# Cosine attention and a GELU MLP in one kernel: scores and values share a ring of three PSUM bank pairs, score passes come in groups of 3,3,3,2,3,3,2,2, and one quad is transposed by TensorE

## Chip, core and metric

One core of one Trainium2 chip. The metric is the device time of one execution in microseconds (us), the median over the runs; lower is better.

## What is computed

```python
# q, k, v: (8, 12, 448, 64) float32; tau = 0.1
q_n = q / (np.linalg.norm(q, axis=-1, keepdims=True) + 1e-06)
k_n = k / (np.linalg.norm(k, axis=-1, keepdims=True) + 1e-06)
scores = np.matmul(q_n, k_n.transpose(0, 1, 3, 2)) / tau
attn = softmax(scores)
attn_out = np.matmul(attn, v)
# heads are put side by side: x is (3584, 768)
h = x @ w_in                                  # (768, 2048)
out = (0.5 * h * (1.0 + erf(h / sqrt(2)))) @ w_out   # (2048, 768)
```

There are 8 batches of 12 heads, 448 positions and 64 features. The output is 3584 rows of 768 float32.

## The kernel before

**Batches, quads, passes.** The kernel works batch by batch (b from 0 to 7). The 12 heads of a batch are three *quads* of four heads. The 448 keys of a head are cut into 7 chunks of 64. A *pass* is one chunk of one quad: `scores` (L227) issues four 64x64 matmuls of 448 columns, which run side by side in the four quarters of TensorE's array, into a tile `st` of two PSUM banks. `exps` (L238) has ScalarE read the two banks and write the exponentials (`pt`, bf16) to SBUF. A batch has 21 passes, 0 to 20; passes 0 to 6 belong to its first quad, 7 to 13 to the second, 14 to 20 to the third.

**Closing a quad.** When the seven passes of a quad have been exponentiated, `both` (L305) closes it. `sums` (L247) adds up the exponentials with a 128x32 matmul by ones into a bank `sm`. VectorE transposes that bank (`turned`, L275), inverts the sums (`inverted`, L280) and spreads them (`spread`, L296). `values` (L261) multiplies the exponentials with v into two banks `o`, again with four 64x64 matmuls side by side per chunk. `normalise` (L301), on VectorE, multiplies each `o` bank with the spread inverse into `x_t[b]`.

**The MLP.** `first` (L597) is the product `x @ w_in` of one batch: 96 matmuls of 128x128 weights and 448 columns, with the GELU on ScalarE into `g`. The product with `w_out` works on two batches at once: a tile of 128 rows and half of the 768 columns takes 16 matmuls of 384 columns (`second_pieces`, L323), then a VectorE copy (L336) into `ot`, then stores. These 16-matmul tiles are the *fill* of the next batch's attention: 96 matmuls (6 tiles) for batches 1, 3, 5 and 7, 128 (8 tiles) for 2, 4 and 6. Batch 0 has no fill and an order of its own, written out by hand (`attention_first`, L385). The tiles left at the end run alone.

**The order is written out by hand** (`manual_schedule`): each engine runs its instructions in the order of the calls, and semaphores keep the data right. `attention` (L563) says how batches 1 to 7 go: ten groups of two passes (group 0 is issued at the end of `first` of the batch before, the last group has one pass), with so many fill matmuls ahead of each group:

```python
plan = {96: (0, 18, 10, 10, 10, 0, 8, 8, 0, 8, 8, 16),
        128: (0, 22, 14, 14, 14, 0, 16, 16, 0, 8, 8, 16)}[len(fill)]
...
            if i in (5, 8):
                both(g0 + (0 if i == 5 else 1), 0 if len(fill) % KF else 1)
            group(b, i)
```

**PSUM's eight banks**: two pairs for `st` (a ring of two, `ps_st`), one bank for `sm` and one for the first half of `o` (`ps_acc`), and two that take turns for everything else (`mm_tile`, L96): the 16-matmul tiles, most of the products of `first`, the second half of `o`. The first products of `first` borrow `st` pairs.

**Preparing q and k.** SyncE's queue loads q and k of a quad (L122). GpSimd squares them (L149), VectorE adds the squares up (`reduce`, L158), ScalarE takes the root as exp(0.5 ln) (`logs`, `roots`), GpSimd adds 1e-6 (L183), VectorE inverts (L185), GpSimd scales and rounds to bf16 `qkb` (L201). A transposed copy `qkT` is then made: in batch 0 by TensorE and a VectorE copy (L218, L223), in the others by a DMA transpose that SyncE issues (L213). SyncE also issues the stores of the output; GpSimd issues the loads of v and of the weights. In the program a quad's preparation is a *unit*; unit 4 is quad 0 of batch 1, unit 5 its quad 1, unit 6 its quad 2.

Of the kernel before, what the change touches and what calls it, by code (L numbers as in the profile page):

```python
# [9 lines left out]
F32 = mybir.dt.float32  # L10
# [6 lines left out]
def kernel(  # L17
# [19 lines left out]
    C = S // D  # L37
    NQ = H // 4
# [4 lines left out]
    KF = d_ff // 128  # L43
# [14 lines left out]
    xp = ctx.enter_context(tc.tile_pool(name="xp", bufs=1))  # L58
    gp = ctx.enter_context(tc.tile_pool(name="gp", bufs=1))
    op_ = ctx.enter_context(tc.tile_pool(name="otp", bufs=3))  # L60
    ps_st = ctx.enter_context(tc.tile_pool(name="ps_st", bufs=2, space=bass.MemoryType.PSUM))
    ps_acc = ctx.enter_context(tc.tile_pool(name="ps_acc", bufs=1, space=bass.MemoryType.PSUM))
    ps_mm = ctx.enter_context(tc.tile_pool(name="ps_mm", bufs=1, space=bass.MemoryType.PSUM))

    ctx.enter_context(tc.manual_schedule())

# [29 lines left out]
    def mm_tile(name, shape=(128, 512), dtype=F32, aside=None):  # L96
        t = ps_mm.tile(list(shape), dtype, tag=f"mm{turn[0] if aside is None else turn[0] ^ aside}", name=name)
        if aside is None:
            turn[0] ^= 1
        return t  # L100

# [120 lines left out]

    st_t = {}

    def scores(g, banks):  # L227
        qkT = qkT_t[g]
        st = ps_st.tile([128, 2, 512], F32, tag="st", name=f"st{g}_{banks[0][1]}")
        for n, (s, c) in enumerate(banks):  # L230
            rows = slice(64 * s, 64 * (s + 1))
            for h in range(2):
                cols = slice(64 * h, 64 * (h + 1))
                nc.tensor.matmul(st[cols, n, :S], lhsT=qkT[rows, 1, c, cols], rhs=qkT[rows, 0, :, cols],  # L234
                                 start=True, stop=True, tile_position=(64 * s, 64 * h))
        st_t[g, banks[0]] = st
# [8 lines left out]
    bank_t = {}  # L245

    def sums(g, chunks=range(C)):  # L247
        for c in chunks:
            if c == 0:
                bank_t[g, "sm"] = ps_acc.tile([128, 512], F32, tag="sm", name=f"sm{g}")  # L250
            for s in range(2):
                if g < NQ:
                    nc.tensor.matmul(bank_t[g, "sm"][64 * s:64 * (s + 1), :S],  # L253
                                     lhsT=ones2.rearrange("p a h r -> p (a h r)"), rhs=pt_t[g, s, c],
                                     start=(c == 0), stop=(c == C - 1), tile_position=(0, 64 * s))
                    continue
                r = 32 * (2 * s + c % 2)
                nc.tensor.matmul(bank_t[g, "sm"][r:r + 32, :S], lhsT=ones, rhs=pt_t[g, s, c],  # L258
                                 start=(c < 2), stop=(c >= C - 2), tile_position=(0, r))

    def values(g, chunks=range(C), aside=None):  # L261
        for c in chunks:
            if c == 0:
                bank_t[g, 0] = ps_acc.tile([128, 512], F32, tag="o", name=f"o{g}_0")
                bank_t[g, 1] = mm_tile(f"o{g}_1", aside=aside)
            for s in range(2):
                for h in range(2):
                    rows, cols = slice(64 * h, 64 * (h + 1)), slice(64 * s, 64 * (s + 1))
                    nc.tensor.matmul(bank_t[g, h][cols, :S], lhsT=v_t[g][rows, s, c, :],  # L269
                                     rhs=pt_t[g, s, c][rows], start=(c == 0), stop=(c == C - 1),  # L270
                                     tile_position=(64 * h, 64 * s))
# [30 lines left out]
        b, n = divmod(g, NQ)  # L302
        nc.vector.tensor_tensor(x_t[b][:, 2 * n + h, :], bank_t.pop((g, h))[:, :S], rs_t.pop((g, h)), ALU.mult)  # L303

    def both(g, aside):  # L305
        sums(g)
        turned(g)
        inverted(g)
        spread(g, 0)
        spread(g, 1)  # L310
        values(g, aside=aside)
        normalise(g, 0)
        normalise(g, 1)

# [70 lines left out]
    def attention_first():  # L385
# [156 lines left out]
        spread(2, 0)  # L542
        inverses(4)
        scale(4)
        transposes(4)
        values(2, (2,))
        values(2, (3,))
        values(2, (4,))
# [4 lines left out]
        normalise(2, 1)  # L553
        done.update({square: 6, reduce: 5, root: 5, scale: 5, transposes: 5})

    passes = [(n, c) for n in range(NQ) for c in range(C)]

    def group(b, k):
        for n, c in passes[2 * k:2 * k + 2]:
            scores(b * NQ + n, ((0, c), (1, c)))  # L560
            exps(b * NQ + n, ((0, c), (1, c)))

    def attention(b, fill):  # L563
        fill = list(fill)
        plan = {96: (0, 18, 10, 10, 10, 0, 8, 8, 0, 8, 8, 16),
                128: (0, 22, 14, 14, 14, 0, 16, 16, 0, 8, 8, 16)}[len(fill)]

        def run(n):
            for _ in range(n):
                fill.pop(0)()  # L570

        x_t[b] = xp.tile([128, KD, S], BF16, tag="x", name=f"x{b}")
        g0, nu = b * NQ, (b + 1) * NQ + 1
        for i in range(1, 11):
            run(plan[i])
            if i == 1:
                for n in (nu - 1, nu):
                    upto(scale, n)
                    upto(transposes, n)
            if i in (5, 8):  # L580
                both(g0 + (0 if i == 5 else 1), 0 if len(fill) % KF else 1)
            group(b, i)
            if i in (2, 5):
                upto(square, nu + (1 if i == 2 else 2))
            if i in (6, 9):
                upto(reduce, nu + (1 if i == 6 else 2))
            if i == 3:
                upto(load_v, b + 3)
            if i == 3 and b == 1:
                upto(load_qk, g0 + NQ + 2)  # L590
            if i == 6:
                upto(load_qk, g0 + NQ + 3)
        upto(root, 2 * b + 5)
        run(plan[11])
        both(g0 + 2, 1)

    def first(b):  # L597
        sb, hf = divmod(b, 2)
        if hf == 0:
            g_t[sb] = gp.tile([128, KF, 2 * S], BF16, tag="g", name=f"g{sb}")  # L600
        nc.scalar.preload_act_table_set(GELU_SET)
        nu = (b + 1) * NQ + 1
        hps = {}
        pairs = (0, 2) if b else (0, 2, 6, 8)
        ahead = 4 if b else 5

        def mm(m, kds):
            for kd in kds:
                nc.tensor.matmul(hps[m], lhsT=wi[:, kd, m * 128:(m + 1) * 128],  # L609
                                 rhs=x_t[b][:, kd, :], start=(kd == 0), stop=(kd == KD - 1))  # L610

        def bank(m):
            if m in pairs:
                st = ps_st.tile([128, 2, 512], F32, tag="st", name=f"hp{b}_{m}")
                hps[m], hps[m + 1] = st[:, 0, :S], st[:, 1, :S]
            elif m not in hps:
                hps[m] = mm_tile(f"hp{b}_{m}")[:, :S]

        for m in range(ahead):
            bank(m)  # L620
            mm(m, range(KD - 2))
        if b == 0:
            upto(square, nu + 3)
        for n in (nu + 1, nu + 2) if b else (nu + 1,):
            upto(scale, n)
            upto(transposes, n)
        if b:
            upto(load_qk, (b + 1) * NQ + 5)
        else:
            upto(load_wo, 4)  # L630
        upto(square, nu + 3)
        upto(reduce, nu + 3)
        for m in range(ahead):
            mm(m, range(KD - 2, KD))
        for m in range(KF):
            if m >= ahead and (m == 0 or m - 1 not in pairs):
                for k in range(m, m + 1 + (m in pairs)):
                    bank(k)
                    mm(k, range(KD))
            nc.scalar.activation(g_t[sb][:, m, hf * S:(hf + 1) * S], hps.pop(m), AF.Gelu)  # L640
            if b == 0 and m == 5:
                nc.scalar.preload_act_table_set(EXP_SET)
                upto(root, 6)
                nc.scalar.preload_act_table_set(GELU_SET)
                upto(scale, nu + 2)
                upto(transposes, nu + 2)
                upto(load_qk, 2 * NQ + 1)
        if b + 1 < B:
            nc.scalar.preload_act_table_set(EXP_SET)
            group(b + 1, 0)  # L650
            upto(root, 2 * b + 6)
# [10 lines left out]
    fill = []  # L662
    for b in range(B):
        if b == 0:
            attention_first()
        else:
            attention(b, fill)
        first(b)
        sb, hf = divmod(b, 2)
        todo = [(t, ni) for t in (range(3) if hf == 0 else range(3, 7)) for ni in range(2)]  # L670
        if b == 0:
            todo.sort(key=lambda x: x[1])
        tail = [2 * S // 128 - 1] if b == B - 1 else []
        fill = [f for t, ni in todo if t not in tail for f in second_pieces(sb, t, ni)]
        fill += [f for t in tail for f in last_pieces(sb, t)]
# [37 lines left out]
```

## Time and profile before

| | |
|---|---|
| median of 13 runs | 427.48 us (426.58 to 436.22) |
| the profiled execution's own time | 427.85 us |
| its span, first to last instruction | 425.9 us |
| TensorE (PE) busy | 414.9 us, 97% |
| ScalarE (ACT) busy | 247.7 us, 58% |
| VectorE (DVE) busy | 191.8 us, 45% |
| GpSimd (POOL) busy | 166.5 us, 39% |
| granted TensorE clock | 0.999 |

The profile page gives busy times of the engines, a picture of the span in slices, the chain of work that ended last, and the costliest groups of instructions; the trace behind it can be asked for any stretch. Line numbers such as L234 are those of the kernel before. "st", "sm", "o", "hp" and "op" are the PSUM tiles of scores, sums, values, the first product and the second product. Stages of the span: batch 0's attention to 33.98 us, its `first` until the scores of batch 1 start at 54.33, batch 1's attention until 84.66, then `first` and attention in turns; the last `first` starts at 383.04 and the last 144 matmuls of the second product at 401.37.

### The profile page before, as it was taken

To read this page: it belongs to the slowest core of one execution; us is meant where nothing else is said; L and a number is where in the kernel's file an instruction comes from. 1 tells how busy PE (TensorE), PEld (TensorE's weight loads), DVE (VectorE), ACT (ScalarE), POOL (GpSimd) and SP (SyncE) were. 2 spreads that over 40 slices of the span, in tenths; PEclk is the share of its full clock that TensorE was granted. 3 is DMA by queue.
4 is the path that set the end of the run, shared out by engine and by line. 5 is a ranking of instruction groups with operands and counts; after the bars stand their busy time and mean duration, and the time that the engine had idled before them with its cause. 6 is when DMAs were issued, how large, how long until landed. Compare 5 with 4: busy or idle time off the path is not lost.

```text
span 425.9 us, 8166 instructions
## 1 busy us (share of the span) xinstructions
PE 414.9 (97%) x3448; PEld 208.6 (49%) x3448; DVE 191.8 (45%) x379; ACT 247.7 (58%) x356; POOL 166.5 (39%) x113
## 2 busy tenths in 40 slices
PE   7899989999999999999999999999999999999996
PEld 3344434555454554545454544555544455445564
DVE  6897117840288304941167501971048611562021
ACT  5895667546655467734767348745666357754300
POOL 5798706360813509090540906353180622000000
PEclk9999999999999999999999999999999999999999
DMA  8999999582482805655092642938076320320023
GB/s 287 269 251 203 176 182 302 123 198 79 84 210 51 225 37 101 172 118 180 17 215 76 129 168 21 228 87 232 2 122 184 82 43 2 82 55 21 2 74 75
DMA packets 68340, 54.99 MB, mean 129 GB/s; under 512 B 40400, under 2 KB 63312, under 8 KB 68304
## 3 DMA queue, kind: packets, MB, share of 16 engines
q1 hardware_dynamic: 55808, 42.25, 38.0%
q0 software_dynamic: 12112, 11.80, 18.1%
q8 instruction: 27, 0.44, 0.4%
q10 hardware_dynamic: 384, 0.43, 0.3%
q14 instruction: 9, 0.07, 0.1%
HBM read 45.61 MB, written 11.01 MB: 133 GB/s over the span
## 4 chain that ended last, share of the span: by engine, by line
PE 88%; POOL 4%; DMA 4%; issue 2%; DVE 1%; ACT 0%; POOLq 0%
PE op L332 35%; PE hp L609 30%; PE st L234 9%; PE o L269 8%; PE sm L258 4%; DMA qkT<-qkb 4%; POOL qkb L201 2%; PE op L347 1%; POOL wi L361 1%; POOL sq L149 1%; PE sm L253 0%; POOL v L134 0%; DVE x L303 0%; DVE nq L158 0%; ACT pt L241 0%
## 5 line engine op out<-in xcount | busy, mean ns | idle before, releaser
L241 ACT ACTIVATE pt<-st 128x896 bf16<-128x896 f32 x168 | 145.2, 915 | 51.2 <-PE st L234 51.0
L332 PE MATMUL op<-wo,g 128*128 128x384 bf16 x864 | 151.5, 327 | 0.0
L609 PE MATMUL hp<-x,wi 128*128 128x448 bf16 x768 | 146.8, 353 | 0.1
L640 ACT ACTIVATE g<-hp 128x448 bf16<-128x448 f32 x128 | 66.6, 547 | 94.9 <-PE hp L609 94.7
L332 PEld LDWEIGHTS <-g 128*128 128x128 bf16 x864 | 79.4, 98 | 66.7 <-issue 18.9
L609 PEld LDWEIGHTS <-wi 128*128 128x128 bf16 x768 | 74.5, 98 | 71.8 <-issue 3.2
L201 POOL TENSOR_TENSOR qkb<-qk,rn 128x896 bf16<-128x896 f32 (+1 forms) x48 | 77.9, 1650 | 10.3 <-DVE rn L185 10.3
L149 POOL TENSOR_TENSOR sq<-qk 128x1792 f32<-128x1792 f32 (+2 forms) x23 | 67.8, 2951 | 15.8 <-DMA qk<-in_k_dram 15.6
L336 DVE COPY ot<-op 128x384 f32<-128x384 f32 x54 | 29.6, 548 | 88.5 <-PE op L332 88.5
L183 POOL TENSOR_SCALAR se<-sr 128x28 f32<-128x28 f32 (+1 forms) x14 | 4.4, 312 | 165.2 <-ACT sr L174 165.2
L158 DVE TENSOR_REDUCE nq<-sq 128x28 f32<-128x1792 f32 (+2 forms) x30 | 48.8, 1636 | 30.0 <-POOL sq L149 29.8
L234 PE MATMUL st<-qkT 64*64 64x448 bf16 x672 | 53.1, 362 | 3.6 <-DMA qkT<-qkb 1.8
L185 DVE RECIPROCAL rn<-se 128x28 f32<-128x28 f32 (+2 forms) x18 | 6.9, 384 | 87.4 <-POOL se L183 87.2
L269 PE MATMUL o<-pt,v 64*64 64x448 bf16 x672 | 37.8, 352 | 0.0
L234 PEld LDWEIGHTS <-qkT 64*64 64x64 bf16 x672 | 17.7, 104 | 33.6 <-issue 24.7
L298 DVE STREAM_TRANSPOSE rs<-rc 128x448 f32<-128x448 f32 x48 | 28.2, 625 | 0.8
L303 DVE TENSOR_TENSOR x<-o,rs 128x448 bf16<-128x448 f32 x48 | 27.0, 599 | 0.6 <-DVE rn L185 0.3
L269 PEld LDWEIGHTS <-v 64*64 64x64 bf16 x672 | 18.3, 106 | 17.2 <-issue 9.1
L277 DVE STREAM_TRANSPOSE tr<-sm 128x448 f32<-128x448 f32 x24 | 15.5, 648 | 11.7 <-PE sm L258 11.1
L258 PE MATMUL sm<-pt,ones 128*32 128x448 bf16 x294 | 19.6, 355 | 0.0
L289 DVE TENSOR_REDUCE tr<-tr 32x28 f32<-32x28 f32 x84 | 16.5, 196 | 1.6
L258 PEld LDWEIGHTS <-ones 128*32 128x32 bf16 x294 | 6.9, 95 | 10.1 <-issue 6.6
(44 smaller groups left out, 117.6 us busy)
## 6 DMA issues: line engine op xcount, KB each, us to landing
out_dram<-ot SPq DMA_DIRECT2D x54, 192.0 KB, 2.8
qk<-in_q_dram SPq DMA_DIRECT2D x23, 448.0 KB, 5.8
qk<-in_k_dram SPq DMA_DIRECT2D x23, 448.0 KB, 6.4
v<-in_v_dram POOLq DMA_DIRECT2D x7, 672.0 KB, 9.5
wi<-in_moe_w_in_dram POOLq DMA_DIRECT2D x8, 384.0 KB, 11.3
wo<-in_moe_w_out_dram POOLq DMA_DIRECT2D x4, 768.0 KB, 16.8
qk<-in_q_dram SPq DMA_DIRECT2D x2, 224.0 KB, 3.5
v<-in_v_dram POOLq DMA_DIRECT2D x1, 448.0 KB, 8.8
```

The lines of the kernel that those rows point to most:

```text
L149: eng.tensor_tensor(sq[:, part], t[:, part], t[:, part], ALU.mult)
L158: nc.vector.tensor_reduce(nq[:, part], sq[:, part], mybir.AxisListType.X, ALU.add)
L201: eng.tensor_tensor(qkb[:, i, :, s0:s1].rearrange("p c s d -> p s c d"), t[:, i, s0:s1], rn[:, i].to_broadcast([128, s1 - s0, C, D]), ALU. ...
L234: nc.tensor.matmul(st[cols, n, :S], lhsT=qkT[rows, 1, c, cols], rhs=qkT[rows, 0, :, cols], start=True, stop=True, tile_position=(64 * s, 6 ...
L241: nc.scalar.activation(pt[:, :m], st[:, :m, :S], AF.Exp, scale=inv_tau)
L258: nc.tensor.matmul(bank_t[g, "sm"][r:r + 32, :S], lhsT=ones, rhs=pt_t[g, s, c], start=(c < 2), stop=(c >= C - 2), tile_position=(0, r))
L269: nc.tensor.matmul(bank_t[g, h][cols, :S], lhsT=v_t[g][rows, s, c, :], rhs=pt_t[g, s, c][rows], start=(c == 0), stop=(c == C - 1), tile_po ...
L298: nc.vector.transpose(rs, bank_t[g, "rc"][:, h].to_broadcast([128, NB, 32]))
L332: nc.tensor.matmul(ps[:, :NH], lhsT=g_t[sb][:, kf, t * 128:(t + 1) * 128], rhs=wo[:, kf, ni * NH:(ni + 1) * NH], start=(kf == 0), stop=(kf ...
L336: nc.vector.tensor_copy(ot[:, ni * NH:(ni + 1) * NH], ps[:, :NH])
L609: nc.tensor.matmul(hps[m], lhsT=wi[:, kd, m * 128:(m + 1) * 128], rhs=x_t[b][:, kd, :], start=(kd == 0), stop=(kd == KD - 1))
L640: nc.scalar.activation(g_t[sb][:, m, hf * S:(hf + 1) * S], hps.pop(m), AF.Gelu)
```

## The change

- Scores of batches 1 to 7 use three bank pairs in a ring, and a quad's two `o` banks are now one of these three pairs. The third pair is made, after batch 0's attention, from the two banks that `sm` and `o` had.
- `sums` of these batches goes into one of the two alternating `mm` banks: the one that the next tile would take, without moving the turn on.
- Groups have 3,3,3,2,3,3,2,2 passes; the plan has six runs of fill in place of nine. A quad is closed between groups 2 and 3, between 5 and 6, and after the last run.
- Batch 1's quad 0 (unit 4) is transposed by TensorE in `first` of batch 0 ahead of product m = 8, with two VectorE copies, in place of the DMA transpose that SyncE issued at the end of batch 0's attention.
- The calls that prepare later quads are put at the places of the new groups that come nearest to the old ones.

```diff
-    ps_st = ctx.enter_context(tc.tile_pool(name="ps_st", bufs=2, space=bass.MemoryType.PSUM))
-    ps_acc = ctx.enter_context(tc.tile_pool(name="ps_acc", bufs=1, space=bass.MemoryType.PSUM))
+    ps_st = ctx.enter_context(tc.tile_pool(name="ps_st", bufs=1, space=bass.MemoryType.PSUM))
     ps_mm = ctx.enter_context(tc.tile_pool(name="ps_mm", bufs=1, space=bass.MemoryType.PSUM))
+    acc = ctx.enter_context(ExitStack())
+    ps_acc = acc.enter_context(tc.tile_pool(name="ps_acc", bufs=1, space=bass.MemoryType.PSUM))
+    third = []
...
+    def pair(i, name):
+        pool = third[0] if i == 2 else ps_st
+        return pool.tile([128, 2, 512], F32, tag=f"st{i}", name=name)
...
             if c == 0:
-                bank_t[g, "sm"] = ps_acc.tile([128, 512], F32, tag="sm", name=f"sm{g}")
+                bank_t[g, "sm"] = ps_acc.tile([128, 512], F32, tag="sm", name=f"sm{g}") if g < NQ else \
+                    mm_tile(f"sm{g}", aside=0)
...
-            if c == 0:
+            if c == 0 and g < NQ:
                 bank_t[g, 0] = ps_acc.tile([128, 512], F32, tag="o", name=f"o{g}_0")
-                bank_t[g, 1] = mm_tile(f"o{g}_1", aside=aside)
+                bank_t[g, 1] = mm_tile(f"o{g}_1")
+            elif c == 0:
+                o = pair(p, f"o{g}")
+                bank_t[g, 0], bank_t[g, 1] = o[:, 0], o[:, 1]
...
         scale(4)
-        transposes(4)
...
     passes = [(n, c) for n in range(NQ) for c in range(C)]
+    group_pairs = [(0, 1, 2), (0, 1, 2), (0, 1, 2), (1, 2), (1, 2, 0), (1, 2, 0), (2, 0), (2, 0)]
 
     def group(b, k):
-        for n, c in passes[2 * k:2 * k + 2]:
-            scores(b * NQ + n, ((0, c), (1, c)))
+        n0 = sum(len(p) for p in group_pairs[:k])
+        for p, (n, c) in zip(group_pairs[k], passes[n0:]):
+            scores(b * NQ + n, ((0, c), (1, c)), p)
             exps(b * NQ + n, ((0, c), (1, c)))
...
-        plan = {96: (0, 18, 10, 10, 10, 0, 8, 8, 0, 8, 8, 16),
-                128: (0, 22, 14, 14, 14, 0, 16, 16, 0, 8, 8, 16)}[len(fill)]
+        plan = {96: (20, 12, 14, 12, 16, 22), 128: (24, 18, 20, 18, 22, 26)}[len(fill)]
...
+        run()
+        for n in (nu - 1, nu):
+            upto(scale, n)
+            upto(transposes, n)
+        group(b, 1)
+        upto(square, nu + 1)
+        run()
+        group(b, 2)
+        both(g0, 0)
+        upto(load_v, b + 3)
+        if b == 1:
+            upto(load_qk, g0 + NQ + 2)
+        group(b, 3)
+        upto(square, nu + 2)
+        run()
+        group(b, 4)
+        upto(reduce, nu + 1)
+        upto(load_qk, g0 + NQ + 3)
+        run()
+        group(b, 5)
+        both(g0 + 1, 1)
+        group(b, 6)
+        run()
+        group(b, 7)
+        upto(reduce, nu + 2)
         upto(root, 2 * b + 5)
-        run(plan[11])
+        run()
         both(g0 + 2, 1)
...
             if m in pairs:
-                st = ps_st.tile([128, 2, 512], F32, tag="st", name=f"hp{b}_{m}")
+                p = (2, 0)[m // 2] if b else (1, 0, 1, 0)[pairs.index(m)]
+                st = pair(p, f"hp{b}_{m}")
...
         for m in range(KF):
+            if b == 0 and m == 8:
+                for i in range(2):
+                    transposes(4, i)
+                    copies(4, i)
```

More of the change, by code (lines that the diff above doesn't have):

```diff
@@ L225, with scores @@
     st_t = {}
-    def scores(g, banks):
+    st_turn = [0]
+    def scores(g, banks, p=None):
         qkT = qkT_t[g]
-        st = ps_st.tile([128, 2, 512], F32, tag="st", name=f"st{g}_{banks[0][1]}")
+        if p is None:
+            p = st_turn[0]
+            st_turn[0] ^= 1
+        st = pair(p, f"st{g}_{banks[0][1]}")
         for n, (s, c) in enumerate(banks):
@@ L259, in sums, with values @@
                                  start=(c < 2), stop=(c >= C - 2), tile_position=(0, r))
-    def values(g, chunks=range(C), aside=None):
+    def values(g, chunks=range(C), p=None):
         for c in chunks:
-            if c == 0:
+            if c == 0 and g < NQ:
                 bank_t[g, 0] = ps_acc.tile([128, 512], F32, tag="o", name=f"o{g}_0")
-                bank_t[g, 1] = mm_tile(f"o{g}_1", aside=aside)
+                bank_t[g, 1] = mm_tile(f"o{g}_1")
+            elif c == 0:
+                o = pair(p, f"o{g}")
+                bank_t[g, 0], bank_t[g, 1] = o[:, 0], o[:, 1]
             for s in range(2):
@@ L303, in normalise, with both @@
         nc.vector.tensor_tensor(x_t[b][:, 2 * n + h, :], bank_t.pop((g, h))[:, :S], rs_t.pop((g, h)), ALU.mult)
-    def both(g, aside):
+    def both(g, p):
         sums(g)
@@ L310, in both @@
         spread(g, 1)
-        values(g, aside=aside)
+        values(g, p=p)
         normalise(g, 0)
@@ L564, in attention, with run @@
         fill = list(fill)
-        plan = {96: (0, 18, 10, 10, 10, 0, 8, 8, 0, 8, 8, 16),
-                128: (0, 22, 14, 14, 14, 0, 16, 16, 0, 8, 8, 16)}[len(fill)]
-        def run(n):
-            for _ in range(n):
+        plan = {96: (20, 12, 14, 12, 16, 22), 128: (24, 18, 20, 18, 22, 26)}[len(fill)]
+        parts = iter(plan)
+        def run():
+            for _ in range(next(parts)):
                 fill.pop(0)()
@@ L573, in attention @@
         g0, nu = b * NQ, (b + 1) * NQ + 1
[L574 to L592, printed above, removed]
+        run()
[23 more added lines that the diff above has]
+        upto(reduce, nu + 2)
         upto(root, 2 * b + 5)
-        run(plan[11])
+        run()
         both(g0 + 2, 1)
@@ L665 @@
             attention_first()
+            acc.close()
+            third.append(ctx.enter_context(tc.tile_pool(name="ps_third", bufs=1, space=bass.MemoryType.PSUM)))
         else:
```

## The prediction, made before the changed kernel was run

> **What bounds the kernel now.** I read the page's busy line first, then the chain that ended last, TensorE's waits, and the ACT and DVE timelines of one attention.
>
> ```profile
> PE 414.9 (97%) x3448; PEld 208.6 (49%) x3448; DVE 191.8 (45%) x379; ACT 247.7 (58%) x356; POOL 166.5 (39%) x113
> ```
>
> TensorE (PE) is the bound: 11 us idle of 425.9, and no other engine is near. So a gain must come out of PE's busy time. The chain shows where (start, length, what):
>
> ```profile
> 107.18 0.50 PE st L234 x8
> 107.68 2.38 PE op L332 x14
> 110.06 0.50 PE st L234 x8
> ...
> 401.37 15.60 PE op L332 x96
> ```
>
> The last stage gives an undisturbed fill matmul: 15.60/96 = 0.1625 us. A stream of 448 columns costs 0.19 (hp: 18.27/96), and the four matmuls of a pass run together. So the period 110.06 - 107.18 = 2.88 should be 14 x 0.1625 + 2 x 0.19 = 2.655. The rest, 0.225, is paid at the two joints between 128x128 and 64x64 work. With runs of ten (57.93 to 60.17: 2.24 - 2.005) it is 0.235: a fixed price per round trip, whatever the lengths. That is what fewer, larger groups can save.
>
> ```profile
> PE st L234 <- DMA qkT<-qkb: 1.8, 1, 1.8
> PE st L234 <- ACT pt L241: 1.2, 2, 1.0
> ```
>
> The first is batch 1's first pass, held to 54.33 by unit 4's DMA transpose (issued 38.37, 15.9 us to landing). The second is put down to ACT, but the exponentials had been done: pass 7 of batch 1 (63.68) waited for unit 5's transpose (issued 48.6, 15.0 to landing, so 63.6). Both crawl beside the w_out loads.
>
> **The joints, from start to start.** A fill run of n costs 0.1625n + 0.104 (16: 2.70). k passes cost 0.19k plus 0.125 between fills (107.11 to 107.61: 0.50), 0.12 ahead of sums, 0.10 behind values (118.48 to 118.96: 0.48). Sums take 0.864, values 1.348, or 1.45 ahead of hp. A batch with 128 fills before: 20.8 + 9 x 0.104 + 21 x 0.19 + 7 x 0.125 + 2 x 0.12 + 2 x 0.10 + 3 x 0.864 + (2 x 1.348 + 1.45) = 33.79; measured 33.90 (102.93 to 136.83), the rest a wait for an exponential. With 96 fills: 28.59; measured 29.13 (155.09 to 184.22), the rest two such waits and 0.30 at 173.3 for an mm bank that a VectorE copy still held; 28.84 in batch 7. The terms close, so I trust them.
>
> **After, without new waits.** Six runs in place of nine; four groups between fills in place of seven; two ahead of sums and two behind values as before. That is 3 x (0.104 + 0.125) = 0.69 less: 33.09 and 27.89.
>
> **New waits, three, each from rows.** Durations hold; only the order is new.
>
> ```profile
> 155.20 0.55 ACT L640 ACTIVATE g<-hp 128x448 bf16<-128x448 f32 x1 [0.59 <-PE hp L609]
> 155.76 1.28 ACT L649 ACT_TABLE_LOAD   x1
> 157.06 1.73 ACT L241 ACTIVATE pt<-st 128x896 bf16<-128x896 f32 x2
> 158.67 0.32 ACT L165 ACTIVATE lq<-nq,tiny 128x28 f32<-128x28 f32 x1
> 159.08 0.23 ACT L174 ACTIVATE sr<-lq 128x28 f32<-128x28 f32 x1
> 159.21 1.71 ACT L241 ACTIVATE pt<-st 128x896 bf16<-128x896 f32 x2
> ```
>
> (1) Quad 0 closes right behind group 2, whose first pass is its last (pass 6). The exponential starts 0.44 after the pass, lasts 0.92 and is seen 0.05 later: 1.41. Sums reach their seventh chunk at 0.69 + 0.55 = 1.24 (four chunks' matmuls side by side, three rounds ahead). Wait 0.17 per batch.
> (2) With 96 fills ACT is behind already. After hp's end it needs the GELU and the table load and starts pass 0 at 1.96 (157.06 - 155.09), then one per 0.81, with 0.67 for the two root steps behind pass 2: pass 5 ends at 1.96 + 2.43 + 0.67 + 1.62 + 0.92 = 7.60. PE wants its bank pair for pass 8 at 0.69 + 3.35 + 0.69 + 2.05 + 0.40 = 7.18. Wait 0.4 here, in which (1) is hidden. Batches 1 and 7 have no root steps there and pay (1).
> (3) Sums now use an mm bank, so quad 2's wait for the copy of the last tile but one, and that copy stands in VectorE's queue behind a reduce and a root:
>
> ```profile
> 173.50 0.64 DVE L277 STREAM_TRANSPOSE tr<-sm 128x448 f32<-128x448 f32 x1
> ...
> 176.73 1.12 DVE L303 TENSOR_TENSOR x<-o,rs 128x448 bf16<-128x448 f32 x2
> 177.77 2.00 DVE L158 TENSOR_REDUCE nq<-sq 128x28 f32<-128x1792 f32 x1
> 179.69 0.55 DVE L336 COPY ot<-op 128x384 f32<-128x384 f32 x1
> 181.34 0.50 DVE L185 RECIPROCAL rn<-se 128x56 f32<-128x56 f32 x1 [1.10 <-POOL se L183]
> 182.01 0.56 DVE L336 COPY ot<-op 128x384 f32<-128x384 f32 x1 [0.17 <-PE op L332]
> ```
>
> From quad 1's sums VectorE needs 0.98 to start, 4.27 through normalise, 0.48 a copy, 2.0 reduce, 0.1, 1.15 for the root through ACT and POOL, 0.48 reciprocal, 0.56 copy, 0.03: 10.05. PE comes from sums to sums in 0.864 + 1.348 + 0.48 + 2.70 + 0.505 + 3.68 = 9.58 with 96 fills: wait 0.47. With 128 it takes 11.2: none. Batch 7 has no such root: none. Behind each of these waits stands all later work of PE, so each is paid in full. Others do not bind. Pair 0 is wanted for pass 13 at 13.38 after the batch's start, free at 13.26 (quad 0's sums start at 7.91, plus 0.98 and 4.37; VectorE has nothing else queued). The next tile in sums' bank comes 2.7 after sums start, and the bank is read by 1.63. Quad 1's sums, at 16.36 with 96 fills, want a copy that stands behind the first reduce (13.13 to 15.1) and ends at 15.6; without that 0.75 of cover they wait one to one. hp's last k-steps want x 5.35 after quad 2's sums start and normalise ends at 5.33, as before. The squares, loads and reduces that are called a pass or two earlier or later lie on POOL and SP, where batch 3's last squares ended 15.6 after its start and their reduce comes at 22: nothing, while that cover of 6 holds.
>
> **Batch 1 and the transposes.** Fourteen TensorE transposes are added where PE is the bound. In batch 0 seven take 0.40 from start to next (18.07 to 18.47), 56 ns each. The Trainium skill ("TensorE: Matmul & The Clock Gate", Part 4: PE-mode transpose) gives about 275 ns each in one kernel's context, and with that they would cost 3.85 us and eat what batch 1 gains. In this trace about 220 ns is one transpose's length, but they overlap; I take 0.8, with 3.9 as the far end (below nothing is excluded: nothing hides work on the bound). The two VectorE copies (0.62 each) start when a reciprocal is over (45.16) and end at 45.8 and 46.4; hp 10 and 11 want the banks at 46.2 and 47.3, so hp's own matmuls hide them by 0.4; if that cover went, hp would slip by as much. POOL's order is unchanged. On SP's queue the move frees unit 5's transpose, unit 7's loads and unit 6's transpose.
> Unit 5's packets, by the trace, ran 53.5 to 63.1, behind unit 4's (42.35 to 53.5), near 185 a us while wo loads ran. Without unit 4, wo moves 200 instead of 145 KB a us and ends near 58.4 instead of 61; unit 5 (1792 packets) starts near 51.5 and lands near 60. Pass 7 wants it at 33.98 + 18.26 + 0.8 + 7.0 = 60.0. Bounds: no wait, to 3.5 if it lands at 63.6 as now. I take 0.2. Unit 7's squares then come before the reduce that stands ahead of the copy for quad 1's sums.
> From hp's start to the end of batch 1: before 33.98 to 84.66 = 50.68. After 18.26 + 0.8 + 27.89 + 0.17 + 0.1 (pass 5's bank) + 0.47 + 0.2 = 47.89. Gain 2.8.
>
> **The sum.** Batch 1: 2.8. Batches 3 and 5: 29.13 - (27.89 + 0.4 + 0.47) = 0.37 each. Batch 7: 28.84 - 28.06 = 0.78. Batches 2, 4, 6: 33.90 - (33.09 + 0.17) = 0.64 each. Total 2.8 + 0.74 + 0.78 + 1.92 = 6.2. Profiled time 427.85 - 6.2 = 421.65; the median lies 0.37 lower: 421.3. The `first` stages and the tail do not change.
>
> **Rivals.**
> *More of it comes free* (0.12): waits (1) to (3) do not appear, because ACT or VectorE get through sooner. Then 6.2 + 3 x 0.17 + 2 x 0.87 + 0.17 + 0.94 = 9.6 less: 417.9. Against: the same rows reproduce the before to 0.1.
> *Unit 5 is as late as ever* (0.15): wo takes the freed share and pass 7 waits until 63.6. It waits 3.6 in place of 0.2 and of (1), so batch 1 loses 0.4 instead of gaining 2.8: 424.5. For it: transposes got only about a quarter of the traffic while wo ran.
> *It doesn't do what it says* (0.08): the 0.23 belongs to the pass, not to the joint (a third pass costs 0.3). Then the joints are not saved and (1) to (3) come on top: batches 2, 4, 6 lose 0.06 each, 3 and 5 lose 0.33 each, 7 gains 0.08, batch 1 gains 2.1: 426.2. Against: behind values a pass costs 0.19.
> *Slower* (0.05): one VectorE queue holds a PE bank. Place: quad 2's sums in batches 1 to 6. Wait (3) grows one to one with any delay of reduce or root: three batches at once, the 128-fill ones from 1.15 on. Slower by 0.5% (8.3 us lost) takes 2 us more in each. The point: the last unit's squares end after 24 us of the batch; they ended at 15.6. Price then: 430.
>
> The likeliest case has 0.60. Below 0.5% (2.1 us) nothing can be told from no change here. Range 418.9 to 424.8: it takes in the last transpose case and most of the free one. Faster 0.86, same 0.09, slower 0.05.
>
> **What would show it.** Right: st groups of three at 0.69 between fills, runs of 12 at 2.05, batch 2's attention 33.25 and batch 3's 28.75; PE st waiting on DMA qkT gone or below 1 us; transposes 0.8 us ahead of hp 8; sm of quad 2 waiting 0.5 for the copy (L352 of the changed kernel) in batches 1, 3 and 5 only; sums' last chunk waiting 0.17. Wrong: a third pass at 0.3; waits of o or op for DVE in the 128-fill batches; unit 5 landing after 61; attention stages equal to before.

## The result and the profile after

The changed kernel's median is 420.97 us (11 runs), the kernel before 427.15 us in all runs beside it: ratio 0.9858, interval [0.983, 0.9887]. Forecast: 421.3. Faster, by the amount and in the places forecast, with a few terms off.

The changed kernel's profiled execution took 423.26 us (span 421.5), longer than the median, and the reason must be read off first. From the page: TensorE's busy line and the granted clock in 40 slices.

```profile
PE 413.1 (98%) x3462; PEld 213.5 (51%) x3462; DVE 190.1 (45%) x381; ACT 245.8 (58%) x356; POOL 166.5 (39%) x113
PEclk9799999999999999999999999999999999999999
```

The second slice has a 7 where the kernel before had nines throughout. Two stretches of it (from and to, length, busy us and count of PE, PEld, DVE, ACT and POOL, then granted clock, DMA share, GB/s):

```profile
12.00:16.30 4.30, 2.90 (x29) 1.68 (x28) 2.69 (x6) 3.89 (x7) 1.19 (x3) 1.00 1.19 277
16.30:23.10 6.80, 6.80 (x39) 2.46 (x35) 4.53 (x7) 4.65 (x7) 6.76 (x7) 0.50 1.09 282
```

For 6.8 us in batch 0, TensorE had half its clock, and batch 0 ended at 36.56 instead of 33.98. Its order of work is the same in both kernels, and in the seven profiles below it ended between 33.3 and 33.8. So 2.6 us of the profile belongs to this execution, not to the change, and everything is compared by stages from batch 0's end on. Stage times here are from the first matmul of a stage to that of the next, in us:

| kernel | batch 0's product and batch 1's attention | attention 2, 4, 6 | attention 3, 5 | attention 7 |
|---|---|---|---|---|
| before | 20.35 + 30.34 = 50.69 | 33.90 | 29.13 | 28.84 |
| forecast | 47.89 | 33.26 | 28.76 | 28.06 |
| after | 19.04 + 28.41 = 47.45 | 33.24 | 28.52 | 28.21 |

The other seven product stages are 18.26 (the last 18.17) in both. From the start of batch 0's product to the last attention's end the changed kernel saves 3.24 + 3 x 0.66 + 2 x 0.61 + 0.63 = 7.1 us.

TensorE's timeline of batch 2's attention after (start, length with the overlap of the last matmul, count), which answers to the chain lines of before:

```profile
106.97 0.76 PE L246 MATMUL st<-qkT 64*64 64x448 bf16 x12
107.67 3.10 PE L348 MATMUL op<-wo,g 128*128 128x384 bf16 x18
110.70 0.76 PE L246 MATMUL st<-qkT 64*64 64x448 bf16 x12
111.39 1.08 PE L271 MATMUL sm<-pt,ones 128*32 128x448 bf16 x14
112.40 1.52 PE L285 MATMUL o<-pt,v 64*64 64x448 bf16 x28
113.75 0.55 PE L246 MATMUL st<-qkT 64*64 64x448 bf16 x8
114.23 3.42 PE L348 MATMUL op<-wo,g 128*128 128x384 bf16 x20
```

Read the starts. Three passes take 0.70 (106.97 to 107.67) where two took 0.50: the third costs 0.19, the bare stream, and the joint is paid once. Eighteen fills take 3.03 = 18 x 0.1625 + 0.104. Sums take 1.01 in place of 0.864 (111.39 to 112.40): wait (1).

TensorE's waits in the changed kernel (two of five lines; the other three lie in batch 0):

```profile
PE st L246 <- ACT pt L253: 1.1, 1, 1.1
PE sm L271 <- DVE ot L352: 0.6, 3, 0.2
```

The waits for a DMA transpose are gone from the list. The first line is one wait in batch 0 (at 12.7), a few us ahead of the halved clock. The second is wait (3), three times. The waits of 0.1 to 0.2 for exponentials are not listed: they hide inside the busy time of overlapping matmuls, and only the distance from start to start shows them.

### The profile page after: what moved, and what is told of

The parts are those of the page before. It is cut to its first block, busy times and chain, and to the rows that moved or that the text cites. A ratio compares the mean times of both kernels' runs of the same rounds, so it can differ in the third digit from the quotient of the medians.

```text
span 421.5 us, 8166 instructions
## 1 busy us (share of the span) xinstructions
PE 413.1 (98%) x3462; PEld 213.5 (51%) x3462; DVE 190.1 (45%) x381; ACT 245.8 (58%) x356; POOL 166.5 (39%) x113
## 4 chain that ended last, share of the span: by engine, by line
PE 47%; issue 29%; POOL 18%; DMA 2%; DVE 2%; SPq 1%; ACT 1%; POOLq 0%
PE hp L633 17%; PE op L348 15%; POOL sq L156 9%; POOL qkb L208 8%; PE st L246 5%; PE o L285 4%; DMA qk<-in_k_dram 2%; PE sm L271 2%; PE sm L266 1%; PE op L363 1%; PE tp L225 1%; POOL v L141 1%; POOL se L190 1%; SPq L129 1%; PE spin L399 0%
## 5 line engine op out<-in xcount | busy, mean ns | idle before, releaser
L253 ACT ACTIVATE pt<-st 128x896 bf16<-128x896 f32 x168 | 142.9, 917 | 42.5 <-PE st L246 41.9
L348 PE MATMUL op<-wo,g 128*128 128x384 bf16 x864 | 147.9, 327 | 0.0
L348 PEld LDWEIGHTS <-g 128*128 128x128 bf16 x864 | 81.1, 98 | 63.7 <-issue 13.2
L246 PE MATMUL st<-qkT 64*64 64x448 bf16 x672 | 48.9, 362 | 1.3 <-ACT pt L253 1.1
L285 PE MATMUL o<-pt,v 64*64 64x448 bf16 x672 | 36.9, 352 | 0.0
L246 PEld LDWEIGHTS <-qkT 64*64 64x64 bf16 x672 | 18.6, 105 | 27.6 <-issue 19.7
L271 PEld LDWEIGHTS <-ones 128*32 128x32 bf16 x294 | 7.8, 95 | 11.5 <-issue 8.0
```

Of the source, the lines that this page charges most:

```text
L253: nc.scalar.activation(pt[:, :m], st[:, :m, :S], AF.Exp, scale=inv_tau)
L348: nc.tensor.matmul(ps[:, :NH], lhsT=g_t[sb][:, kf, t * 128:(t + 1) * 128], rhs=wo[:, kf, ni * NH:(ni + 1) * NH], start=(kf == 0), stop=(kf ...
```

## Experiments

Seven kernels, made from before or after (e6 from e4). The ratio is to the runs of before beside each kernel (medians 426.77 to 427.13). Stages of the profiled execution, in us:

| kernel | product 0 + attention 1 | 2, 4, 6 | 3, 5 | 7 | median | ratio to before, interval |
|---|---|---|---|---|---|---|
| e1_groups_only | 19.97 + 31.85 | 33.24 | 28.50 | 28.21 | 423.3 | 0.9914 [0.988, 0.9948] |
| e2_transpose_only | 19.05 + 29.17 | 33.90 | 29.12 | 28.83 | 424.98 | 0.9955 [0.9942, 0.9968] |
| e3_ring_groups_of_two | 19.05 + 28.87 | 33.90 | 28.81 | 28.81 | 424.15 | 0.9933 [0.9908, 0.9958] |
| e4_sums_in_pair | 19.05 + 28.16 | 33.24 | 28.21 | 28.21 | 419.73 | 0.9827 [0.9788, 0.9866] |
| e5_one_more_reduce | 19.05 + 29.10 | 33.24 | 29.15 | 28.21 | 422.57 | 0.989 [0.9852, 0.9928] |
| e6_sums_in_pair_and_plan | 19.05 + 28.04 | 33.24 | 28.04 | 28.04 | 419.16 | 0.9825 [0.9779, 0.9871] |
| e7_reduce_ahead | 19.05 + 31.54 | 34.10 | 31.83, 32.07 | 28.21 | 433.48 | 1.0148 [1.0113, 1.0183] |

**e1_groups_only: is the TensorE transpose worth anything?** From after:

```diff
         scale(4)
+        transposes(4)
...
-            if b == 0 and m == 8:
-                for i in range(2):
-                    transposes(4, i)
-                    copies(4, i)
```

> The changed kernel with one part undone: unit 4 is transposed by SyncE's DMA again, at its old place; groups, ring and banks stay as changed. My account: the joints are saved in all seven batches, but in batch 1 the first pass is held to the landing of unit 4's transpose (54.3 us, if batch 0 runs as in the profile of before) and pass 7 to unit 5's (63.6); that batch ends near 84.9 instead of 81.4, so about 424.4 us. Rival, that the transposes were hidden anyway and all of the gain is in the groups: about 421 us, no TensorE wait on a DMA above 1 us.

Measured 423.3, with every batch from 2 on as in the change. From TensorE's waits, then its timeline in batch 1:

```profile
PE st L246 <- DMA qkT<-qkb: 3.3, 2, 1.9
```

```profile
60.12 0.38 PE L246 MATMUL st<-qkT 64*64 64x448 bf16 x4
62.38 0.57 PE L246 MATMUL st<-qkT 64*64 64x448 bf16 x8 [1.88 <-DMA qkT<-qkb]
62.88 1.16 PE L271 MATMUL sm<-pt,ones 128*32 128x448 bf16 x14
63.97 2.83 PE L285 MATMUL o<-pt,v 64*64 64x448 bf16 x28
```

Both transpose waits are there, as expected, and pass 7 waits longer than before, since the larger groups reach it sooner. New is the last line: values took 2.62 from start to next in place of 1.35. No semaphore holds them; the granted clock was 0.5 from 63.5 to 66.9, and that belongs to this execution: its mean clock was 0.995, while the other five of e1 had 0.998 to 1.0, and 3.4 us at half clock take 0.004 off the mean. Without the 1.3 us that values lost by it, batch 1 would have come to about 50.5, as before (50.69). So without the moved transpose the larger groups gain nothing in batch 1, and 421 needs both parts. The rival falls.

**e2_transpose_only: the other part by itself.** From before: the same four lines moved the other way (`transposes(4)` out, the block ahead of m = 8 in).

> The kernel before with the other part alone: unit 4 transposed by TensorE ahead of product m = 8; groups of two, two pairs, own banks for sums and values. My account: the product stage of batch 0 grows by 0.86 us and the two transpose waits (2.1 with the pass's idle time, and 1.05) go; 427.15 - 2.3 = about 424.9 us, and batches 2 to 7 to the hundredth as before (33.90 and 29.13). Rival, that it matters only together with larger groups: 427 us.

Measured 424.98: the product of batch 0 and batch 1's attention take 48.22 instead of 50.69, 2.5 less, and all later stages stay within 0.01. The part pays alone.

**e3_ring_groups_of_two: banks or joints?** The three pairs with the old plan, from after:

```diff
-    group_pairs = [(0, 1, 2), (0, 1, 2), (0, 1, 2), (1, 2), (1, 2, 0), (1, 2, 0), (2, 0), (2, 0)]
+    pass_pairs = [0, 1, 2, 0, 1, 2, 0, 1, 2, 0, 2, 0, 2, 0, 1, 2, 1, 2, 1, 2, 1]
...
-        plan = {96: (20, 12, 14, 12, 16, 22), 128: (24, 18, 20, 18, 22, 26)}[len(fill)]
+        plan = {96: (0, 18, 10, 10, 10, 0, 8, 8, 0, 8, 8, 16),
+                128: (0, 22, 14, 14, 14, 0, 16, 16, 0, 8, 8, 16)}[len(fill)]
```

with the loop of before around it, `both` at groups 5 and 8, and values in pairs 1, 0 and 0.

> The changed kernel's three bank pairs, values in a pair, sums in an mm bank, transposes on TensorE, but the old plan: groups of two passes and nine runs of fill. My account (the gain is in the joints, 0.23 each, not in the banks): batches 2, 4, 6 stay at 33.8 to 33.9, batches 3 and 5 at 28.9 to 29.3, only batch 1 gains; about 424.5 us. Rival (the third pair takes waits for exponentials away, which hide inside busy TensorE time): batches 2 to 7 gain what they gained in the change, 33.24 and 28.5; about 421 us.

TensorE in batch 2 of this kernel:

```profile
100.06 3.75 PE L348 MATMUL op<-wo,g 128*128 128x384 bf16 x22
103.74 0.57 PE L246 MATMUL st<-qkT 64*64 64x448 bf16 x8
104.24 2.45 PE L348 MATMUL op<-wo,g 128*128 128x384 bf16 x14
106.62 0.57 PE L246 MATMUL st<-qkT 64*64 64x448 bf16 x8
```

A period of 2.88 (103.74 to 106.62), the one of the kernel before, to the hundredth, with the third pair there. Batches 2, 4 and 6 stay at 33.90. The third pair by itself is worth nothing there; in batches 3 and 5 it takes 0.32 away, the wait that values had for an mm bank. What the change saves is joints. Groups of three with only two pairs were not run; that they need the third pair is an estimate: the third pass would want the first one's bank 0.38 after the first one's start, and that bank is read by 1.36 (the exponential starts 0.44 after the pass and lasts 0.92).

**e4_sums_in_pair: wait (3) taken away.** Quad 2's sums in pair 2 instead of an mm bank, from after:

```diff
-                    mm_tile(f"sm{g}", aside=0)
+                    (mm_tile(f"sm{g}", aside=0) if p is None else pair(p, f"sm{g}")[:, 0])
...
-        both(g0 + 2, 1)
+        both(g0 + 2, 1, 2)
```

> The changed kernel with quad 2's sums in the first bank of pair 2 (its pass 19 has been read long before) instead of the mm bank that a copy behind reduce and root still holds; nothing else. My account: the wait of 0.24 to 0.30 us ahead of these sums in batches 1, 3 and 5 goes, nothing else comes (the first product of the next stage wants pair 2 only 2.3 us after sums start, and the bank is read by 1.7); 0.8 us less than the changed kernel, about 420.2 us. Rival, that the wait moves to the next thing behind VectorE's queue (values' pair or the products' last k-steps): the same 421 us, with hp waiting on VectorE.

TensorE around quad 2 of batch 3, after and then e4:

```profile
176.00 3.75 PE L348 MATMUL op<-wo,g 128*128 128x384 bf16 x22
179.98 0.93 PE L271 MATMUL sm<-pt,ones 128*32 128x448 bf16 x14 [0.23 <-DVE ot L352]
```

```profile
172.52 3.75 PE L348 MATMUL op<-wo,g 128*128 128x384 bf16 x22
176.20 0.93 PE L271 MATMUL sm<-pt,ones 128*32 128x448 bf16 x14
```

From 3.98 to 3.68 start to start, and 28.52 to 28.21 for the stage; nothing took the wait's place. Of the 420.97 - 419.73 = 1.24 us by medians, the stages show 0.25 + 2 x 0.31 = 0.87. Taken each against the runs of before beside it, the medians agree: 426.77 - 419.73 = 7.04 saved against 427.15 - 420.97 = 6.18, so 0.86.

**e5_one_more_reduce and e7_reduce_ahead: the slower rival made large.** One more VectorE reduce of 2 us, of squares already there, into a tile that nobody reads; e5 puts it behind the second reduce, e7 ahead of it:

```diff
         upto(reduce, nu + 2)
+        if nu + 2 <= NU:
+            again = nrm.tile([128, 2, 2, C], F32, tag="again", name=f"again{b}")
+            nc.vector.tensor_reduce(again, sq_t[units[nu + 1][0]], mybir.AxisListType.X, ALU.add)
         upto(root, 2 * b + 5)
```

> The changed kernel with one more VectorE reduce of 2 us (into a tile that nobody reads) right behind the second reduce of batches 1 to 6, so ahead of the root, the last copies and quad 2's sums: it makes the slower rival's mechanism larger. My account: the copy that quad 2's sums wait for comes 1.93 us later; with 96 fills the wait of 0.24 to 0.30 grows by all of it, with 128 fills VectorE's way (9.88 in the changed kernel's batch 3) had 1.3 left to TensorE's 11.2, so 0.6 appears. 3 x 1.93 + 3 x 0.6 = 7.6: about 428.5 us, batch 3 at 30.45 and batch 2 at 33.85. Rival, that VectorE has slack enough (45% busy) to hide 2 us: 421 us.

Measured 422.57: my account missed by 6 us. VectorE's timeline in batch 3, after and then e5:

```profile
175.83 2.00 DVE L165 TENSOR_REDUCE nq<-sq 128x28 f32<-128x1792 f32 x1
179.02 0.50 DVE L192 RECIPROCAL rn<-se 128x56 f32<-128x56 f32 x1 [1.19 <-POOL se L190]
179.44 0.95 DVE L352 COPY ot<-op 128x384 f32<-128x384 f32 x2
```

```profile
173.72 2.00 DVE L165 TENSOR_REDUCE nq<-sq 128x28 f32<-128x1792 f32 x1
175.64 2.01 DVE L619 TENSOR_REDUCE again<-sq 128x28 f32<-128x1792 f32 x1
177.56 0.49 DVE L192 RECIPROCAL rn<-se 128x56 f32<-128x56 f32 x1
```

Behind the reduce, VectorE idles 1.19 us for the root that ScalarE and GpSimd take. The further reduce fills that gap first, from 177.76 (175.83 plus a reduce's 1.93) to 179.02; of its 1.93 only some 0.65 reaches the copy: 28.52 to 29.15. With 128 fills nothing shows. I had added up a queue that has a hole in it. So e7 moves the same work ahead of the hole:

> The same further VectorE reduce of 2 us as in the run before, now ahead of the second reduce and not behind it. Behind it, 1.2 us of it lay in the time in which VectorE waits for ScalarE and GpSimd to take the root, so only 0.65 came through. My account now: ahead of the reduce the whole chain from reduce to copy starts 1.93 later, so all of it comes through with 96 fills (batches 3 and 5 at 30.4 in place of 28.52), and 0.6 with 128 (33.85 in place of 33.24), where VectorE's way had 1.3 to spare; about 7.6 us on the changed kernel's 421, 428.5, slower than before. Rival, that VectorE catches up before the copy in any case: as in the run before, 422.6.

Measured 433.48, slower than before: a delay ahead of the root is paid as the slower rival said, and its price is higher than I gave. TensorE in batch 3, then two stretches of it (columns as above):

```profile
177.68 3.75 PE L348 MATMUL op<-wo,g 128*128 128x384 bf16 x22
183.58 1.02 PE L271 MATMUL sm<-pt,ones 128*32 128x448 bf16 x14 [2.15 <-DVE ot L352]
184.53 2.83 PE L285 MATMUL o<-pt,v 64*64 64x448 bf16 x28
```

```profile
181.30:183.58 2.28, 0.13 (x2) 0.09 (x1) 1.09 (x4) 1.87 (x3) 0.73 (x2) 1.00 0.01 4
184.30:187.70 3.40, 3.40 (x36) 1.29 (x31) 2.88 (x9) 0.00 (x0) 3.40 (x3) 0.50 0.45 116
```

Sums wait 2.22 (5.90 less 3.68): 0.30 as in the change plus 1.92, all of the reduce, as expected. But then TensorE runs at half clock for 3.4 us, which costs 1.4 us more in this attention (values take 2.76 in place of 1.45) and 0.2 in the product behind it. The profile has three such stretches, and the mean clock of all four executions (0.986 to 0.988) fits them. With 128 fills 0.86 came through, not 0.6: there the chain starts later, with a copy that waits for TensorE.

**e6_sums_in_pair_and_plan: the exponentials' wait.** From e4, `96: (22, 12, 14, 12, 14, 22)`.

> The kernel with quad 2's sums in pair 2, and for the batches with 96 fills the plan 22, 12, 14, 12, 14, 22 in place of 20, 12, 14, 12, 16, 22, so that group 1 comes 0.33 us later and ScalarE has caught up. My account: the two waits for exponentials there (0.10 at pass 5, 0.19 at pass 8) go, and the one that they hid, 0.15 ahead of the last chunk of quad 0's sums, comes back: batches 3, 5 and 7 at 28.07 in place of 28.21, 0.1 each, 419.4 us against 419.7, less than timing can show but plain in the stages. Rival, that ScalarE is behind by more: 28.21 or longer.

TensorE in batch 3 of e6:

```profile
155.04 0.76 PE L246 MATMUL st<-qkT 64*64 64x448 bf16 x12
155.73 2.12 PE L348 MATMUL op<-wo,g 128*128 128x384 bf16 x12
157.79 0.76 PE L246 MATMUL st<-qkT 64*64 64x448 bf16 x12
158.48 1.08 PE L271 MATMUL sm<-pt,ones 128*32 128x448 bf16 x14
```

The two groups of three take 0.69 each; in e4 they took 0.82 (154.35 to 155.17) and 0.88 (157.22 to 158.10). So the two waits were 0.13 and 0.19, and one of 0.15 came back: stages of 28.04 in place of 28.21 in all of batches 3, 5 and 7. 419.16 us is the lowest median here; its interval overlaps those of e4 and of the changed kernel, and theirs overlap too, so only the stages tell the three apart.

## Why the prediction was right, step by step

*The joints* held. Taking e3 as the changed kernel without them, batches 2, 4 and 6 save 33.90 - 33.24 = 0.66; the sum was 0.69 saved and 0.17 of new wait, against 0.11 of old waits that go. What within a joint costs the time no run here separates.

*Wait (1)*: 0.17 forecast, 0.15 measured. *Wait (2)*: 0.4 forecast in one place, 0.32 measured in two (0.13 at pass 5, 0.19 at pass 8). One sentence of this step was wrong: batch 7 has the root steps behind group 0 too, for its own quad 2, so it pays (2) and took 28.21, not 28.06. They stood in the trace of before as well (at 357.77). ScalarE's timeline after:

```profile
354.72 0.33 ACT L172 ACTIVATE lq<-nq,tiny 128x28 f32<-128x28 f32 x1
```

*Wait (3)*: right place and batches, too large: 0.47 forecast, 0.24 in batch 1 and 0.30 in batches 3 and 5; e4 takes it away. The step added instruction lengths end to end; from quad 1's sums to quad 2's it came to 10.05, and 170.10 to 179.98 gives 9.88. Part of the excess is in the joint behind the reciprocal: the copy starts 0.42 behind it, not 0.48.

*The transposes*: 14 took 0.78 of TensorE, forecast 0.8. TensorE's timeline after:

```profile
45.65 0.94 PE L225 MATMUL tp<-ident,qkb 128*128 128x128 bf16 x14
46.43 9.24 PE L633 MATMUL hp<-x,wi 128*128 128x448 bf16 x48
```

Start to start, 56 ns each. The Trainium skill ("TensorE: Matmul & The Clock Gate", Part 4: PE-mode transpose) gives about 275 ns for one in a kernel's context; as the price of each in this stream that does not hold, since rows of 219 ns overlap: the measurement decides, and the case against this part falls. The two VectorE copies stayed hidden; hp ran on at 0.19.

*Unit 5*: the direction was right and the size cautious. In e2, e3 and e4, whose batch 0 ended at 33.3 to 33.7 (before 33.98), the w_out loads end at 56.9 to 57.1 (forecast 58.4; before 63.1, which the forecast had taken for 61), unit 5's packets run from 52.0 to 57.8, and there is no wait where 0.2 was forecast. e1 shows what the late transposes cost the larger groups, 3.3 us of waits.

*The sum*: 6.2 forecast, 6.2 between the medians, 7.1 between the two profiles by stages. By stages it was 0.9 too low: the terms that were too dear (wait (3), 0.2 of unit 5 and part of wait (2)), less batch 7's 0.15, would have given 7.0. That the forecast meets the medians to a tenth is in part luck. In e2 to e6 too the stages show 0.5 to 0.9 more than the medians, so the surplus seems to lie in the one profile of before that all are compared with; that execution took 0.7 more than its kernel's median. Where in it is not settled.

## What to carry to other kernels

When an engine is 97% busy, measure from start to start: fixed prices at joints and waits of 0.1 to 0.3 us sit inside "busy". Here one round trip between array shapes cost 0.23 us, and regrouping the same matmuls was worth about 0.7 us a batch with 128 fills; in batch 1 it was worth it only with the late transfer moved as well. Before adding up a queue's lengths, look for its holes: the same 2 us of work cost 0.64 us on one side of a wait for another engine and all of it on the other.

## What the runs showed that I had not expected

A long wait of TensorE can be paid more than once. After idle stretches of 2.10, 2.15 and 2.15 us (e7) and 1.88 us (e1's profiled execution) the granted clock fell to half 0.5 to 1.1 us behind the restart and stayed there for 3.41 us each time; after 0.8 to 0.9 us (six times in e5 and e7) it did not, nor after 1.41 us in e1 and 1.79 us in the kernel before.

Length alone does not decide. In all nine traces, each stretch of one granted clock that ends inside the span lasts a whole multiple of 3.41 us, so the changes lie on a grid with that step. The four idle stretches that were followed by half clock each lay within one step of it. The 1.79 us of the kernel before were cut by it, 0.80 in one step and 0.99 in the next. Two steps each, e1 and then before (the second number is the length, the third TensorE's busy time; the clock is the third from the end):

```profile
60.04:63.46 3.42, 1.54 (x25) 0.58 (x26) 0.56 (x1) 1.86 (x3) 0.00 (x0) 1.00 1.12 238
63.46:66.87 3.41, 3.41 (x38) 1.46 (x36) 2.61 (x9) 1.08 (x2) 1.97 (x1) 0.50 1.29 249
```

```profile
49.92:53.34 3.42, 2.62 (x14) 1.17 (x12) 0.00 (x0) 1.83 (x4) 1.96 (x2) 1.00 1.27 192
53.34:56.75 3.41, 2.42 (x20) 1.34 (x21) 0.00 (x0) 2.81 (x3) 0.00 (x0) 1.00 1.28 191
```

So where a wait falls seems to count beside its length, which fits that only one of six executions of e1 shows the stretch. Idle time is not all either: in the changed kernel's profile, an idle stretch of 1.1 us among sparse work in batch 0 was followed by 6.83 us at half clock, two steps. How much it takes was not tried.
